# Smaller last additions, landing waits on GpSimd and another closing barrier in a fused SSM and FFN kernel

## The chip, the cores and the metric

The kernel runs on one core of one Trainium2 chip. The metric is device time in microseconds (us) of one execution.

Numbers in ns are starts and durations of the trace's instruction records. "Landing" means the last of the completion events of a store's semaphore in the trace. The profile's views round the same records to 0.01 or 0.1 us.

## The reference, cut to what matters

```
xn = layernorm(x)                                   # x: 2048 x 512, bf16
out = x + ssm(xn) + (silu(xn @ w_gate) * (xn @ w_up)) @ w_down
# ssm: complex diagonal recurrence over the 2048 rows (512 states), then
#      y = 2 * Re(h @ C^T) + xn * Dskip
```

The output is 2048 x 512 in bf16. The kernel handles the rows in four chunks of 512, each of four row tiles of 128.

## The kernel before: the parts that the change and the argument touch

A small scheduler orders tasks for five engines: `pe` (TensorE), `dve` (VectorE), `act` (ScalarE), `pool` (GpSimd) and `sp` (SyncE, which issues nearly all DMAs). The last function computes a chunk's output. For each row tile TensorE accumulates 11 matmuls of the FFN (`mmA`) and 8 of the SSM (`mmB`) in one PSUM bank, VectorE adds the bank to the residual, and SyncE stores the result. In the last chunk the fourth tile is cut in two pieces of 256 columns.

```python
def dc_chunk(c, mid=None, split_last=False):
    ...
    for lt in range(4):
        if split_last and lt == 3:
            items.append((lt, 0, 256))
            items.append((lt, 256, 256))
        else:
            items.append((lt, 0, 512))
    ...
    for (lt, c0, nc_), bk in zip(items, banks):   # mmA: 11 matmuls, hT x wd
        ...
    for (lt, c0, nc_), bk in zip(items, banks):   # mmB: 8 matmuls, hss x W12
        ...
        g.add("dve", lambda e, ...: e.tensor_tensor(out=x_sb[:, a, c0:c0 + nc_],
              in0=pbank[:, bk, 0:nc_], in1=x_sb[:, a, c0:c0 + nc_], op=ALU.add), ...)
        dma("st_out%d_%d" % (a, c0), out_v[:, a, c0:c0 + nc_], x_sb[:, a, c0:c0 + nc_], ...)
```

At the end each engine's stream is emitted into a block. SyncE also waits for every output's landing, and the block closes with a barrier of all engines.

```python
block = es.enter_context(nc.Block())
...
@block.sync
def _(e):
    _emit(e, streams["sp"])
    for t in streams["sp"]:
        if t.out:
            e.wait_ge(t.sem, 16)
...
@block.gpsimd
def _(e):
    _emit(e, streams["pool"])
```

## Time and profile before

| Kernel before | |
|---|---|
| time, median of 3 runs | 180.56 us (180.40 to 181.02) |
| profiled span | 178.8 us |
| TensorE, VectorE busy | 98%, 90% |
| last matmul's end to the span's end ("the tail") | 2.489 us |

The page of the kernel before gives the span, the engines' busy shares (line of its part 1) and, by engine, the chain of waits that ended last (line of its part 4). PE is TensorE's matmuls, PEld its weight loads, DVE VectorE, ACT ScalarE, POOL GpSimd and SP SyncE; a q behind a name is that engine's instruction queue.

```profile
span 178.8 us, 2346 instructions
...
PE 174.5 (98%) x908; PEld 82.9 (46%) x908; DVE 160.6 (90%) x272; ACT 86.5 (48%) x107; POOL 13.0 (7%) x24
...
PE 95%; DMA 2%; ACTq 1%; ACT 0%; DVE 0%; issue 0%
```

TensorE is the chain, nearly from start to end. Of the lines that follow, L713 is the FFN's gate and up matmuls, L900 is `mmA`, L913 `mmB` and L918 the additions; after the change, L901, L914 and L919. An ending can be shortened only behind its last matmul, so that is where to look. The timeline of the kernel before from 176.2 us (start, duration, engine, line, operation, and in brackets the idle time before it and what ended that):

```profile
175.93 1.20 SPq L385 DMA_DIRECT2D out_dram<-x_sb  x2
175.93 0.38 PE L913 MATMUL pb<-W,hss 128*128 128x256 bf16 x2
176.35 0.42 DVE L918 TENSOR_TENSOR x_sb<-pb,x_sb 128x256 bf16<-128x256 f32 x1 [0.45 <-PE pb L913]
```

The last matmul ends at 175.93 + 0.38 = 176.31 us. The last addition follows at 176.35 and takes 0.42 us. The second of the two stores ends its issue at 175.93 + 1.20 = 177.13 us. What follows is in the instructions of SyncE's landing waits (L986) and of the block's close (L272); columns are durations in ns (min/median/max), then the first and last start in us:

```profile
L986 SPq EVENT_SEMAPHORE  x8: 27/28/28, 177.2 to 178.4; - x8
```

```profile
L272 POOLq EVENT_SEMAPHORE  x2: 17/17/17, 178.6 to 178.7; - x2
L272 POOLq DRAIN  x1: 1431/1431/1431, 75.3 to 75.3; - x1
...
L272 SPq COMPARE_BRANCH  x1: 33/33/33, 178.4 to 178.4; - x1
L272 SPq DRAIN  x1: 7/7/7, 178.6 to 178.6; - x1
...
L272 PEldq EVENT_SEMAPHORE  x1: 51/51/51, 178.8 to 178.8; - x1
```

The view lists groups, not an order. In order of time: SyncE's last landing wait ends at 178.4, its branch out of the block follows, its drain at 178.6, GpSimd gathers the engines' signals (178.6) and releases them (178.7), and the others leave by 178.8. GpSimd's own drain is recorded at 75.3 us, where its program ends. Its 1431 ns span GpSimd's last operation (75.37 to 76.70 us in the records), and nobody waits for it.

### The profile page before, as it was taken

The page shows a single profiled execution, that of the slowest core. Times are in us where ns is not written, and L with a number is a line of the kernel's source. Part 1 is how long each engine was busy: PE and PEld are TensorE (multiplying, and loading weights), DVE is VectorE, ACT ScalarE, POOL GpSimd, SP SyncE. Part 2 cuts the span into 40 slices and gives each one's busy share as a digit, 9 for nine tenths or more (in the row PEclk, how much of TensorE's full clock was granted, in tenths as well). Part 3 has the DMA queues.
Part 4 walks back from the last instruction along what each step waited for, and adds up shares of the span by engine and source line. Part 5 has one row for each costly group of instructions (what it writes and reads, how often), then busy time and mean ns, then how long its engine had stood idle before and what let it go on. Part 6 is the DMA issues. An engine that isn't in the chain of part 4 may idle for free.

```text
span 178.8 us, 2346 instructions
## 1 busy us (share of the span) xinstructions
PE 174.5 (98%) x908; PEld 82.9 (46%) x908; DVE 160.6 (90%) x272; ACT 86.5 (48%) x107; POOL 13.0 (7%) x24
## 2 busy tenths in 40 slices
PE   8799999999999999999999999999999999999994
PEld 2594444444444444444444444444444444444643
DVE  3888759998799999999999999999999999999733
ACT  3379899899696992060565651000965620000000
POOL 3362300001300000210000000000000000000000
DMA  5995646669360000002330000001100000001212
GB/s 159 353 355 110 129 81 72 148 170 354 113 117 4 0 0 0 0 0 92 85 64 0 0 0 4 0 0 59 59 0 4 0 0 0 0 0 33 69 48 88
DMA packets 23410, 12.37 MB, mean 69 GB/s; under 512 B 15112, under 2 KB 23400, under 8 KB 23400
## 3 DMA queue, kind: packets, MB, share of 16 engines
q1 hardware_dynamic: 22832, 11.70, 24.6%
q10 hardware_dynamic: 568, 0.53, 1.0%
q8 instruction: 7, 0.11, 0.3%
q14 instruction: 3, 0.02, 0.0%
HBM read 6.46 MB, written 2.10 MB: 48 GB/s over the span
## 4 chain that ended last, share of the span: by engine, by line
PE 95%; DMA 2%; ACTq 1%; ACT 0%; DVE 0%; issue 0%
PE pb L713 36%; PE pb L900 21%; PE pb L913 15%; PE pb L818 15%; PE pb L752 3%; DMA wg<-in_B_w_gate_dram 2%; PE pb L781 2%; PE pb L791 1%; ACTq L385 1%; PE pb L543 0%; ACT xnT L549 0%; DVE x_sb L918 0%; PE pb L457 0%
## 5 line engine op out<-in xcount | busy, mean ns | idle before, releaser
L858 DVE TENSOR_TENSOR_SCAN rot<-sm,car,rot 128x512 bf16<-128x512 f32 x32 | 39.1, 1268 | 0.1
L900 PE MATMUL pb<-wd,hT 128*128 128x512 bf16 (+3 forms) x187 | 38.7, 367 | 0.0
L713 PE MATMUL pb<-xnT,wu 128*128 128x512 bf16 x160 | 37.3, 379 | 0.0
L713 PE MATMUL pb<-xnT,wg 128*128 128x512 bf16 x136 | 32.0, 380 | 0.0
L913 PE MATMUL pb<-W,hss 128*128 128x512 bf16 (+1 forms) x136 | 28.3, 367 | 0.0
L818 PE MATMUL pb<-xnT,BT 128*128 128x512 bf16 x128 | 28.1, 379 | 0.0
L900 PEld LDWEIGHTS pb<-wd,hT 128*128 128x128 bf16 (+1 forms) x187 | 18.2, 97 | 20.1
L725 ACT ACTIVATE sg<-pb 128x1024 bf16<-128x1024 f32 x20 | 20.2, 1021 | 10.5 <-PE pb L713 10.2
L713 PEld LDWEIGHTS pb<-xnT,wu 128*128 128x128 bf16 x160 | 15.5, 98 | 18.9 <-ACT uf L771 0.5
L771 ACT ACTIVATE uf<-pb 128x1024 bf16<-128x1024 f32 x20 | 20.4, 1021 | 7.1 <-PE pb L713 5.7
L713 PEld LDWEIGHTS pb<-xnT,wg 128*128 128x128 bf16 x136 | 13.1, 98 | 16.4 <-issue 0.8
L913 PEld LDWEIGHTS pb<-W,hss 128*128 128x128 bf16 x136 | 13.3, 98 | 14.4
L818 PEld LDWEIGHTS pb<-xnT,BT 128*128 128x128 bf16 x128 | 12.5, 98 | 15.1
L825 ACT ACTIVATE u_sb<-pb 128x1024 bf16<-128x1024 f32 x16 | 16.3, 1025 | 3.9 <-PE pb L818 3.5
L918 DVE TENSOR_TENSOR x_sb<-pb,x_sb 128x512 bf16<-128x512 f32 (+1 forms) x17 | 10.9, 655 | 5.0 <-PE pb L913 5.0
L773 DVE TENSOR_TENSOR hT<-sg,uf 128x1024 bf16<-128x1024 bf16 x20 | 13.4, 677 | 2.1 <-ACT uf L771 2.1
L466 DVE BATCH_NORM_STATS2 st<-x_sb 128x6 f32<-128x512 bf16 x16 | 10.2, 681 | 5.0 <-DMA x_sb<-in_A_x_dram 5.0
L495 ACT ACTIVATE xn_sb<-x_sb,nmr,rstd 128x512 bf16<-128x512 bf16 x8 | 5.9, 802 | 10.5 <-DVE nmr L492 10.5
L800 ACT ACTIVATE sg<-pb 96x1024 bf16<-96x1024 f32 x2 | 2.0, 1019 | 17.4 <-PE pb L781 17.4
L849 DVE TENSOR_TENSOR rot<-rot,sin 128x2048 bf16<-128x2048 bf16 x8 | 9.8, 1219 | 0.0
L849 DVE TENSOR_TENSOR rot<-u_sb,sin 128x2048 bf16<-128x2048 bf16 x8 | 9.7, 1218 | 0.0
L849 DVE TENSOR_TENSOR rot<-u_sb,cosT 128x2048 bf16<-128x2048 bf16 x8 | 9.7, 1215 | 0.0
(71 smaller groups left out, 138.8 us busy)
## 6 DMA issues: line engine op xcount, KB each, us to landing
out_dram<-x_sb SPq DMA_DIRECT2D x15, 128.0 KB, 1.7
x_sb<-in_A_x_dram SPq DMA_DIRECT2D x3, 512.0 KB, 7.5
wd<-in_B_w_down_dram SPq DMA_DIRECT2D x1, 1280.0 KB, 7.0
wu<-in_B_w_up_dram SPq DMA_DIRECT2D x1, 768.0 KB, 6.1
wg<-in_B_w_gate_dram SPq DMA_DIRECT2D x1, 608.0 KB, 7.5
wu<-in_B_w_up_dram SPq DMA_DIRECT2D x1, 608.0 KB, 8.6
x_sb<-in_A_x_dram SPq DMA_DIRECT2D x4, 128.0 KB, 2.8
wg<-in_B_w_gate_dram ACTq DMA_DIRECT2D x2, 256.0 KB, 3.8
```

Of the source, the lines that this page charges most:

```text
L466: return g.add("dve", lambda e, a=a: e.bn_stats(out=st[:, a, :], in_=x_sb[:, a, :]), reads=[("x", a)], writes=[("st", a)], name="bnst%d" % ...
L713: inst = e.matmul(pbank[0:fs, bk, :].rearrange("p (j t) -> p j t", j=4), lhsT=w[:, kt, i * 128:i * 128 + fs], rhs=xnT[:, c % 2, :, kt, :], ...
L725: g.add("act", lambda e: e.activation(out=sg[rows, sl, 0:n, :].rearrange("p a t -> p (a t)"), in_=pair_f32(rows, bk, 512 * n), func=AF.Sil ...
L771: g.add("act", lambda e: e.activation(out=uf[rows, ul, 0:n, :].rearrange("p a t -> p (a t)"), in_=pair_f32(rows, bk, 512 * n), func=AF.Ide ...
L773: g.add("dve", lambda e: e.tensor_tensor(out=hT[rows, hb, i0:i0 + n, :], in0=sg[rows, sl, 0:n, :], in1=uf[rows, ul, 0:n, :], op=ALU.mult), ...
L818: inst = e.matmul(pbank[:, bk, :].rearrange("p (j t) -> p j t", j=4), lhsT=BT[:, ri, kt, pt * 128:(pt + 1) * 128], rhs=xnT[:, c % 2, :, kt ...
L825: g.add("act", lambda e: e.activation(out=u_sb[:, us].rearrange("p r t -> p (r t)"), in_=pair_f32(slice(0, 128), b0), func=AF.Identity), r ...
L849: tt = lambda out, a, b, op, r, w, nm: g.add("dve", lambda e: e.tensor_tensor(out=out, in0=a, in1=b, op=op), reads=r, writes=w, name="%s_% ...
L858: g.add("dve", lambda e, A0=A0, A1=A1, k=k, ri=ri, pt=pt: e.tensor_tensor_scan(out=A1[:, k, ri, :], data0=rr[:, pt:pt + 1].to_broadcast([1 ...
L900: inst = e.matmul(pbank[:, bk, 0:nc_], lhsT=hT[0:fs, hb, i, lt * 128:(lt + 1) * 128], rhs=wd[0:fs, i, c0:c0 + nc_], start=(i == 0), stop=F ...
L913: inst = e.matmul(pbank[:, bk, 0:nc_], lhsT=hss[:, hb, pt, ri, lt * 128:(lt + 1) * 128], rhs=W12[:, ri, pt, c0:c0 + nc_], start=False, sto ...
L918: g.add("dve", lambda e, bk=bk, a=a, c0=c0, nc_=nc_: e.tensor_tensor(out=x_sb[:, a, c0:c0 + nc_], in0=pbank[:, bk, 0:nc_], in1=x_sb[:, a, ...
```

## The change

Three intents: shorten the last addition, from 256 to 128 columns; let GpSimd, which is idle and anyway runs the barrier, wait for the landings; and close the block with the barrier that uses semaphores only and leaves GpSimd's drain out. The last 256 columns are still stored by one DMA.

```diff
-        block = es.enter_context(nc.Block())
+        block = es.enter_context(nc.Block(no_gpsimd_drain=True))
...
-                    items.append((lt, 256, 256))
+                    items.append((lt, 256, 128))
+                    items.append((lt, 384, 128))
...
-                dma("st_out%d_%d" % (a, c0), out_v[:, a, c0:c0 + nc_], x_sb[:, a, c0:c0 + nc_], ...)
+                if nc_ == 128 and c0 == 256:
+                    continue
+                d0, dn = (256, 256) if nc_ == 128 else (c0, nc_)
+                dma("st_out%d_%d" % (a, d0), out_v[:, a, d0:d0 + dn], x_sb[:, a, d0:d0 + dn], ...)
...
         @block.sync
         def _(e):
             _emit(e, streams["sp"])
-            for t in streams["sp"]:
-                if t.out:
-                    e.wait_ge(t.sem, 16)
...
         @block.gpsimd
         def _(e):
             _emit(e, streams["pool"])
+            for t in streams["sp"]:
+                if t.out:
+                    e.wait_ge(t.sem, 16)
```

(Cuts: the estimates that the scheduler uses, and the other engines' streams, which only move in the text.)

More of the change, by code (lines that the diff above doesn't have):

```diff
@@ L902, in dc_chunk @@
                 g.add("pe", mmA, reads=[("hT", hb, i) for i in range(FT)] + [("wd", 0), ("wd", 1)],
-                      writes=BK(bk), name="mm_dA%d_%d" % (4 * c + lt, c0), est=FT * (216 if nc_ == 512 else 110), ninst=FT)
+                      writes=BK(bk), name="mm_dA%d_%d" % (4 * c + lt, c0), est=FT * (216 if nc_ == 512 else nc_ * 0.43), ninst=FT)
             if mid is not None:
@@ L916, in dc_chunk @@
                 g.add("pe", mmB, reads=[("hss", hb, pt) for pt in range(PT)] + [("W", ri, pt) for ri in range(2) for pt in range(PT)],
-                      writes=BK(bk), name="mm_dB%d_%d" % (a, c0), est=2 * PT * (216 if nc_ == 512 else 110), ninst=2 * PT)
+                      writes=BK(bk), name="mm_dB%d_%d" % (a, c0), est=2 * PT * (216 if nc_ == 512 else nc_ * 0.43), ninst=2 * PT)
                 g.add("dve", lambda e, bk=bk, a=a, c0=c0, nc_=nc_: e.tensor_tensor(out=x_sb[:, a, c0:c0 + nc_], in0=pbank[:, bk, 0:nc_], in1=x_sb[:, a, c0:c0 + nc_], op=ALU.add),
-                      reads=BK(bk) + [("x", a)], writes=[("xo", a, c0)], name="oadd%d_%d" % (a, c0), est=(660 if nc_ == 512 else 360))
-                dma("st_out%d_%d" % (a, c0), out_v[:, a, c0:c0 + nc_], x_sb[:, a, c0:c0 + nc_], writes=[("out", a, c0)], nbytes=TILEB * nc_ // 512, reads=[("xo", a, c0)], out_=True)
+                      reads=BK(bk) + [("x", a)], writes=[("xo", a, c0)], name="oadd%d_%d" % (a, c0), est=(660 if nc_ == 512 else 100 + nc_))
+                if nc_ == 128 and c0 == 256:
+                    continue
+                d0, dn = (256, 256) if nc_ == 128 else (c0, nc_)
+                dma("st_out%d_%d" % (a, d0), out_v[:, a, d0:d0 + dn], x_sb[:, a, d0:d0 + dn], writes=[("out", a, d0)], nbytes=TILEB * dn // 512,
+                    reads=[("xo", a, c) for c in ((256, 384) if nc_ == 128 else (c0,))], out_=True)
         if _CFG["warm"]:
```

## The prediction

> **What bounds the kernel now.** The page of before: TensorE is busy 98% of a 178.8 us span; the chain of waits is 95% TensorE; the granted clock is 1.000 (view of cores). The change touches only the tail. From the timeline of the last 10 us, the chain, the barrier line's instructions and the DMA view:
>
> - the last 256-column matmul ends near 176.31 us;
> - the last addition, 128x256, runs 176.35 to 176.77 (0.42 us);
> - its store is issued at 176.8 (0.33 us of queue time) and lands some 1.5 us later (median of the two 64 KB stores); SyncE's last wait ends at 178.4;
> - then SyncE's branch (33 ns), drain (7 ns, at 178.6) and barrier signal, GpSimd's gather and release (178.6, 178.7), and the other engines' release up to 178.8. So about 0.4 us lies between landing and end.
>
> Of the 180.56 us, 1.8 us lie outside the span; I expect them unchanged.
>
> **What the change does, costed.**
>
> 1. *Smaller last addition.* Additions took 0.69 us (512 columns) and 0.425 us (256); a line through both gives 0.29 us for 128 (estimate). The first 128-column one starts 0.45 us before the last matmul ends and is done in time, so the chain loses 0.42 - 0.29 = 0.13 us.
> 2. *More, smaller matmuls.* 19 matmuls of 256 columns become 38 of 128. In before's chain the 256-column ones cost 109.8 ns each (9.54 us less 33 of 215.9 ns, over 22), the 128-column ones of the first stage 55.8 ns (40 in 2.23 us). Each split costs 1.8 ns: +0.03 us. The Trainium skill, "TensorE: Matmul & The Clock Gate", Part 1, gives a warm gap of about 56 ns for 128 columns; this trace agrees.
> 3. *One store of 256 columns, as before.* No change, but 0.1 us sooner.
> 4. *VectorE's order.* The compiled order moves the third chunk's second addition (0.69 us) ahead of the two that write hss. These end near 165.4 instead of 164.8; TensorE needs them at 169.4. The sixth piece's new bank wait is for that moved addition (done near 163.1), over 5 us early. No cost.
> 5. *Waits on GpSimd.* GpSimd is idle after 76.7 us; only the last landing counts. SyncE's branch, drain, signal and the hop to GpSimd leave the chain: I estimate 0.1 to 0.2 us of the 0.4.
> 6. *No GpSimd drain in the barrier.* It took 1.43 us, but at 75.3 us, overlapping GpSimd's last operation: hidden, so no gain. (After the change it would stand behind the landing waits; skipping it avoids a loss.)
>
> Sum: -0.13 + 0.03 - 0.15 = -0.25 us, all on the critical path, 0.14% of the whole. **Predicted 180.3 us, 8 in 10 between 179.9 and 180.65. Faster by over 2%: 0.01; within 2%: 0.98; slower by over 2%: 0.01.**
>
> **What would show each step.** 1: the last two additions at 0.29 us each, the last within 0.05 us of the last matmul's end. 2: 128-column matmuls 55 to 57 ns apart, TensorE's end within 0.1 us of 176.3. 3: landing about 1.5 us after issue. 5: 0.2 to 0.3 us from landing to the span's end, no SyncE instruction in between. 6: no GpSimd drain in the tail.
>
> **What would make it wrong.** GpSimd noticing a landing later than SyncE; the semaphore-only barrier having more hops; a narrow addition having a larger fixed cost than the line says; the time outside the span moving. The spread of before (180.4 to 181.02) is as large as the gain.

## The result, and the profile after

| | before | after |
|---|---|---|
| median of 6 runs, first comparison | 180.70 us | 180.26 us |
| ratio, 95% interval | | 0.9977 [0.9961, 0.9993] |
| profiled span | 178.801 us | 178.432 us |
| tail behind the last matmul | 2.489 us | 2.344 us |

The ratios are from runs of the same rounds. All of them lie within 0.0005 of the ratio of the mean times, but they are not the ratios of the medians quoted.

The page of the changed kernel, same lines:

```profile
span 178.4 us, 2380 instructions
...
PE 174.3 (98%) x919; PEld 83.6 (47%) x927; DVE 160.8 (90%) x273; ACT 86.5 (48%) x107; POOL 12.7 (7%) x24
...
PE 95%; DMA 1%; DVE 1%; issue 1%; ACT 0%; POOL 0%
```

Its timeline from 175.45 us:

```profile
175.23 0.74 DVE L919 TENSOR_TENSOR x_sb<-pb,x_sb 128x256 bf16<-128x256 f32 x2 [0.18 <-PE pb L914]
175.25 0.83 PE L914 MATMUL pb<-W,hss 128*128 128x128 bf16 x12
...
175.69 1.09 SPq L385 DMA_DIRECT2D out_dram<-x_sb  x2
176.12 0.29 DVE L919 TENSOR_TENSOR x_sb<-pb,x_sb 128x128 bf16<-128x128 f32 x1 [0.15 <-PE pb L914]
```

VectorE is idle 0.15 us before the last addition, so the first 128-column addition was indeed done in time. The last one takes 0.29 us instead of 0.42. The close of the changed kernel, GpSimd's landing waits (L1007) and the block's end:

```profile
L1007 POOLq EVENT_SEMAPHORE  x8: 43/43/43, 164.3 to 178.0; - x8
```

```profile
L272 PEldq EVENT_SEMAPHORE  x2: 51/51/51, 176.2 to 178.4; - x2
...
L272 POOLq EVENT_SEMAPHORE  x2: 17/17/17, 178.2 to 178.3; - x2
...
L272 SPq DRAIN  x1: 128/128/128, 176.8 to 176.8; - x1
L272 POOLq COMPARE_BRANCH  x1: 33/33/33, 178.1 to 178.1; - x1
```

No GpSimd drain is left, and SyncE's drain moved up to 176.8. But the branch didn't vanish: it stands at 178.1 on GpSimd now, and the order wait, branch, gather, release is the same as before. From the last landing to the span's end the records give 463 ns before and 457 ns after.

The whole difference of the two spans can be split at points in the records:

| Stretch | before, us | after, us | difference, ns |
|---|---|---|---|
| start to the first matmul of L713 | 13.055 | 12.986 | -69 |
| from there to the last chunk's outputs | 146.620 | 146.410 | -210 |
| the last chunk's matmuls (last stages of L900 and L913; L901 and L914 after) | 16.637 | 16.692 | +55 |
| tail | 2.489 | 2.344 | -145 |
| span | 178.801 | 178.432 | -369 |

Only the last two stretches hold changed instructions: -145 + 55 = -90 ns. The other -279 ns are in unchanged parts. The -210 ns come from one stall of TensorE in the profiled run of before, in the waits of 49 to 52 us (who waited for whom, us in total, times, longest):

```profile
PEld pb L713 <- ACT uf L771: 0.5, 1, 0.5
```

The profile of after has no such line in that stretch. Whether that is chance or a consequence of the change is the first thing to test.

### The profile page after: what moved, and what is told of

Its sections match the earlier page's. It is cut to its first block, busy times and chain, and to the rows that moved or that the text cites. A ratio compares the mean times of both kernels' runs of the same rounds, so it can differ in the third digit from the quotient of the medians. Undisturbed runs are those within 1.5% of the kernel's fastest.

```text
span 178.4 us, 2380 instructions
## 1 busy us (share of the span) xinstructions
PE 174.3 (98%) x919; PEld 83.6 (47%) x927; DVE 160.8 (90%) x273; ACT 86.5 (48%) x107; POOL 12.7 (7%) x24
## 4 chain that ended last, share of the span: by engine, by line
PE 95%; DMA 1%; DVE 1%; issue 1%; ACT 0%; POOL 0%
PE pb L713 36%; PE pb L901 21%; PE pb L818 15%; PE pb L914 15%; PE pb L752 3%; PE pb L781 2%; DMA x_sb<-in_A_x_dram 1%; PE pb L791 1%; PE pb L543 1%; DVE st L466 0%; ACT xnT L549 0%; POOL rstd L478 0%; PE pb L450 0%; DVE xn_sb L485 0%; DVE x_sb L919 0%
## 5 line engine op out<-in xcount | busy, mean ns | idle before, releaser
L901 PE MATMUL pb<-wd,hT 128*128 128x512 bf16 (+3 forms) x194 | 38.1, 355 | 0.2
L713 PE MATMUL pb<-xnT,wu 128*128 128x512 bf16 x160 | 37.3, 379 | 0.0
L713 PE MATMUL pb<-xnT,wg 128*128 128x512 bf16 x136 | 32.0, 379 | 0.0
L914 PE MATMUL pb<-W,hss 128*128 128x512 bf16 (+2 forms) x140 | 28.1, 355 | 0.2
L901 PEld LDWEIGHTS pb<-wd,hT 128*128 128x128 bf16 (+1 forms) x198 | 18.5, 98 | 19.9
L713 PEld LDWEIGHTS pb<-xnT,wu 128*128 128x128 bf16 x160 | 15.6, 98 | 18.6
L713 PEld LDWEIGHTS pb<-xnT,wg 128*128 128x128 bf16 x136 | 13.2, 98 | 16.4 <-issue 0.8
L914 PEld LDWEIGHTS pb<-W,hss 128*128 128x128 bf16 x144 | 13.5, 98 | 14.3
L919 DVE TENSOR_TENSOR x_sb<-pb,x_sb 128x512 bf16<-128x512 f32 (+2 forms) x18 | 10.9, 621 | 4.9 <-PE pb L914 4.9
```

The source lines that it names most:

```text
L713: inst = e.matmul(pbank[0:fs, bk, :].rearrange("p (j t) -> p j t", j=4), lhsT=w[:, kt, i * 128:i * 128 + fs], rhs=xnT[:, c % 2, :, kt, :], ...
L901: inst = e.matmul(pbank[:, bk, 0:nc_], lhsT=hT[0:fs, hb, i, lt * 128:(lt + 1) * 128], rhs=wd[0:fs, i, c0:c0 + nc_], start=(i == 0), stop=F ...
L914: inst = e.matmul(pbank[:, bk, 0:nc_], lhsT=hss[:, hb, pt, ri, lt * 128:(lt + 1) * 128], rhs=W12[:, ri, pt, c0:c0 + nc_], start=False, sto ...
L919: g.add("dve", lambda e, bk=bk, a=a, c0=c0, nc_=nc_: e.tensor_tensor(out=x_sb[:, a, c0:c0 + nc_], in0=pbank[:, bk, 0:nc_], in1=x_sb[:, a, ...
```

## The experiments

Theory A: the tail gain is the shorter addition alone, the new ending is worth nothing, and the rest of the measured gain is chance in the kernel's first third. Theory B, the prediction's: the ending is worth another 0.1 to 0.2 us.

All tails, in ns, from the records. They add up from left to right.

| Run | matmul end to last addition | last addition | addition end to issue | issue to landing | landing to end | tail |
|---|---|---|---|---|---|---|
| before | 37 | 425 | 28 | 1536 | 463 | 2489 |
| before_again | 37 | 425 | 28 | 1537 | 463 | 2490 |
| end_only | 38 | 425 | 27 | 1534 | 457 | 2481 |
| split_only | 37 | 291 | 28 | 1536 | 458 | 2350 |
| after | 37 | 292 | 28 | 1530 | 457 | 2344 |
| after_again | 38 | 293 | 28 | 1532 | 466 | 2357 |
| pool_drain | 38 | 291 | 28 | 1534 | 540 | 2431 |
| sp_semonly | 37 | 290 | 27 | 1533 | 542 | 2429 |
| late_wait | 38 | 293 | 28 | 1532 | 68 | 1959 |
| late_again | 37 | 292 | 28 | 1531 | 67 | 1955 |
| late_two_stores | 38 | 293 | 116 | 1534 | 67 | 2048 |
| narrow64 | 80 | 214 | 27 | 1527 | 466 | 2314 |
| late_narrow | 78 | 215 | 28 | 1532 | 67 | 1920 |

All outputs are right.

### split_only: the smaller additions alone

```diff
 # against the changed kernel
-        block = es.enter_context(nc.Block(no_gpsimd_drain=True))
+        block = es.enter_context(nc.Block())
 # and the landing waits back from GpSimd to SyncE
```

> Only the smaller additions; landing waits stay on SyncE and the barrier keeps GpSimd's drain. The tail from TensorE's last matmul end to the span's end took 2.489 us in the kernel before and 2.344 us in the changed one. Theory A (the whole tail gain is the shorter last addition, 0.425 to 0.292 us): tail 2.34 to 2.37 us, that is 0.12 to 0.15 less than before; about 0.46 us from the last landing to the span's end. Theory B (my prediction: moving the waits and the barrier is worth another 0.1 to 0.2 us): this kernel keeps most of the old ending, tail at or above 2.44 us. Both expect a time within 0.2% of the kernel before, and 128-column matmuls 55 to 57 ns apart.

Measured: tail 2.350 us, landing to end 0.458 us, 180.76 us median of 4 runs, ratio 1.0003 [0.9971, 1.0035]. The last addition, from the timeline of this run:

```profile
176.67 0.29 DVE L919 TENSOR_TENSOR x_sb<-pb,x_sb 128x128 bf16<-128x128 f32 x1 [0.15 <-PE pb L914]
```

With the old ending in place, 139 of the 145 ns are there. Theory A holds in the trace.

### end_only: the new ending alone

```diff
 # against the kernel before
-        block = es.enter_context(nc.Block())
+        block = es.enter_context(nc.Block(no_gpsimd_drain=True))
 # and the landing waits from SyncE to GpSimd; pieces stay 256 and 256
```

> Only the ending: landing waits on GpSimd and the semaphore-only barrier; two pieces of 256 columns as in the kernel before. Theory A: tail 2.47 to 2.50 us, no gain against 2.489; from the last landing to the span's end 0.45 to 0.47 us as before (0.463). Theory B: tail 2.29 to 2.39 us, landing to end 0.26 to 0.36 us.

Measured: tail 2.481 us (8 ns less than before), landing to end 0.457 us, ratio 0.9995 [0.9963, 1.0028]. Theory B falls. The landing waits (L1002) and the branch are on GpSimd here, as in the changed kernel:

```profile
L1002 POOLq EVENT_SEMAPHORE  x8: 43/43/43, 168.7 to 178.7; - x8
```

```profile
L272 POOLq COMPARE_BRANCH  x1: 32/32/32, 178.8 to 178.8; - x1
```

This run also shows the stall near 50 us, in the waits of 40 to 60 us:

```profile
PEld pb L713 <- ACT uf L771: 0.9, 1, 0.9
...
PE pb L713 <- ACT uf L771: 0.4, 1, 0.4
```

So the stall comes with the new ending too, and the second profile of the kernel before (below) doesn't have it. Two runs of one program show it best: late_again (below) has the 0.5 us wait and a middle that is 0.21 us longer, and late_wait, the same program, has a wait of 0.4 us and only 0.035 us. The stall goes with the run, not with the kernel. What brings it on was not investigated.

### pool_drain: landing waits on GpSimd, ordinary barrier

```diff
 # against the changed kernel
-        block = es.enter_context(nc.Block(no_gpsimd_drain=True))
+        block = es.enter_context(nc.Block())
```

> The changed kernel with the ordinary barrier: landing waits on GpSimd, followed by GpSimd's drain. Both theories expect the drain to appear at the tail now, behind the last landing wait, instead of hidden near 75 us. If the drain waits only for GpSimd's own old work it costs under 0.1 us there (tail 2.34 to 2.44 us); if it has a large cost of its own, as its 1.43 us record near 75 us might suggest, the tail is 0.5 us longer or more.

Measured: tail 2.431 us, ratio 0.9995 [0.9968, 1.0021]. Of the block's close:

```profile
L272 POOLq COMPARE_BRANCH  x1: 41/41/41, 178.1 to 178.1; - x1
L272 POOLq DRAIN  x1: 46/46/46, 178.2 to 178.2; - x1
```

The drain is now at the end and costs 540 - 457 = 83 ns from landing to end (74 against the 466 of after_again, whose branch took 41 ns as here), of which its own record is 46. The 1431 ns at 75.3 us were GpSimd's unfinished work, not a price of the drain.

### sp_semonly: landing waits on SyncE, semaphore-only barrier

```diff
 # against the changed kernel: only the waits move back
         @block.sync
         def _(e):
             _emit(e, streams["sp"])
+            for t in streams["sp"]:
+                if t.out:
+                    e.wait_ge(t.sem, 16)
```

> The changed kernel with the landing waits back on SyncE, the semaphore-only barrier kept. Theory A: the two engines are alike as waiters; tail 2.34 to 2.42 us, the difference being SyncE's drain and one more hop to GpSimd, of 0.03 to 0.07 us. Theory B: the tail is 0.1 to 0.2 us longer than the changed kernel's 2.344, that is 2.44 to 2.54 us.

Measured: tail 2.429 us, ratio 1.0001 [0.9974, 1.0027]. Both ranges are narrowly missed: theory A's ended at 2.42, theory B's began at 2.44. From landing to end it took 542 ns, 79 more than with the ordinary barrier on the same engine (463). First the line of SyncE's semaphore instructions in the kernel before (only its release), then the lines of the close of this run (the signal at 178.5, and the release):

```profile
L272 SPq EVENT_SEMAPHORE  x1: 17/17/17, 178.7 to 178.7; - x1
```

```profile
L272 SPq EVENT_SEMAPHORE  x2: 17/17/17, 178.5 to 178.6; - x2
...
L272 SPq COMPARE_BRANCH  x1: 33/33/33, 178.3 to 178.3; - x1
L272 SPq DRAIN  x1: 7/7/7, 178.4 to 178.4; - x1
```

By the records' operands, SyncE's drain itself raises the gather's semaphore in the ordinary barrier. In the semaphore-only barrier a separate semaphore instruction does so; it starts 60 ns after the drain's end and ends 77 ns after it. That is the 79 ns, within 2.

The four corners, landing to end in ns, now explain why the new ending gained nothing (540 and 542 are one profile each):

| | ordinary barrier | semaphore-only barrier |
|---|---|---|
| SyncE waits | 463, 458, 463 | 542 |
| GpSimd waits | 540 | 457, 457, 466 |

Each half of the change alone loses about 80 ns, for different reasons: a drain that is no longer hidden, or a signal that no longer rides on the drain. The two together lose neither and come back to where the kernel before was. Step by step, again in ns:

| Step | before | after |
|---|---|---|
| landing to the end of the wait's record | 45 | 67 |
| to the end of the branch's record | 73 | 77 |
| to GpSimd's gather | 162 | 128 |
| gather, release, other engines leave | 183 | 185 |

SyncE's drain, signal and hop to GpSimd were worth only 162 - 128 = 34 ns, and GpSimd gives 26 of those back in its own wait and branch.

### after_again: the changed kernel once more

> The changed kernel once more. Theory A (the tail is fixed, and what moves from run to run is the head): tail 2.34 to 2.35 us and 0.45 to 0.46 us from landing to end, as in the first profile; TensorE's last stage takes the same time within 0.02 us; the span may differ by up to 0.6 us, all of it before TensorE's last stages. The ratio to the kernel before lies between 0.998 and 1.0005: 0.145 us gained in the tail less 0.055 us lost in the smaller matmuls is 0.09 us or 0.05%. Theory B (the first comparison's 0.23% is real): ratio 0.996 to 0.9985.

Measured: tail 2.357 us, landing to end 0.466 us, last chunk's matmuls 16.691 us (16.692 the first time), 180.80 us median of 6 runs, ratio 0.9998 [0.9978, 1.0019]. Theory A's range for the ratio holds; the 0.23% of the first comparison doesn't come back. Three of its narrower ranges were missed, each by little: the tail (2.34 to 2.35), landing to end (0.45 to 0.46) and the span, which was to differ by up to 0.6 us. The span was 179.132 us, 0.700 more than the first profile of the very same program. Of that, 0.687 us lie before the first matmul of L713 (13.673 instead of 12.986 us), while the inputs load.

### before_again: the kernel before once more

> The kernel before once more, profiled again, since its tail is known from one profile alone. Theory A (the tail is fixed, the head moves): tail from TensorE's last end to the span's end 2.47 to 2.50 us (2.489 in the first), landing to end 0.455 to 0.47 us; the second pieces' 256-column matmuls 109 ns apart. Theory B (the tail of before varies as much as its times do, by 0.5 us or more): tail outside 2.40 to 2.58. The ratio to itself lies within 0.2% of 1; what it shows beyond that is chance.

Measured: tail 2.490 us, landing to end 0.463 us, last chunk's matmuls 16.637 us, to the nanosecond as before. From the first matmul of L713 to the last matmul's end it took 163.048 us instead of 163.257: the stall of 0.21 us is absent. The changed kernel took 163.102 us in that stretch, in both of its profiles. So the unchanged middle of the two kernels is equal, and the 54 to 55 ns between them are those of the last chunk's smaller matmuls. The ratio of this kernel to itself was 0.9989 [0.9967, 1.0012], which shows what chance does here.

### late_wait: the last two landing waits behind the barrier

The branch and the barrier need 0.39 us, but no data from the last store. So they can run while it is in flight.

```diff
 # against the changed kernel; outs = the output stores in order of issue
         @block.gpsimd
         def _(e):
             _emit(e, streams["pool"])
-            for t in streams["sp"]:
-                if t.out:
-                    e.wait_ge(t.sem, 16)
+            for t in outs[:-2]:
+                e.wait_ge(t.sem, 16)
+
+    for t in outs[-2:]:                    # after the block is closed
+        nc.gpsimd.wait_ge(t.sem, 16)
```

> The changed kernel, with the waits for the last two output landings moved from inside the block to behind its barrier (still on GpSimd, so nothing ends before the data has landed). Four profiles so far put 0.457 to 0.463 us between last landing and span's end where the ending is whole, nearly all of it branch and barrier. Theory A (the barrier can run while the store is in flight): barrier done near 1.2 us after TensorE's end, landing to end 0.06 to 0.12 us, tail 1.93 to 2.00 us instead of 2.344, and the time 0.2 to 0.3% below the kernel before, ratio 0.9965 to 0.9985. Theory B (the end of the run waits for something the span doesn't show, as the 1.76 us outside the span suggest): the span shrinks by the 0.39 us but the time outside it grows by as much, and the ratio stays at 0.9985 to 1.001.

Measured: tail 1.959 us, landing to end 0.068 us, 180.14 us median of 6 runs against 180.86 of before in the same rounds, ratio 0.9965 [0.9942, 0.9987]. The trace accounts for 530 - 51 = 479 ns, or 0.27%, of that 0.35%, well inside the interval. The landing wait (L1011) and the close:

```profile
L1011 POOLq EVENT_SEMAPHORE  x1: 43/43/43, 178.5 to 178.5; - x1
```

```profile
L272 POOLq EVENT_SEMAPHORE  x2: 17/17/17, 177.5 to 177.6; - x2
...
L272 POOLq COMPARE_BRANCH  x1: 41/41/41, 177.3 to 177.3; - x1
```

The barrier is over by 177.7 us, the data lands at 178.43, one semaphore instruction ends the span. Outside the span this kernel spends 1.74 to 1.81 us (in late_again), the kernel before 1.69 to 1.77 (in before_again): 0.05 us more on average (0.03 against the other runs of before in these rounds), not the 0.39 that theory B expected. The spans of these executions are on record to 0.1 us only.

### late_two_stores: and the last 256 columns in two stores

```diff
 # against late_wait: every piece has its own store, also those of 128 columns
-                if nc_ == 128 and c0 == 256:
-                    continue
-                d0, dn = (256, 256) if nc_ == 128 else (c0, nc_)
 # and the last three landings are awaited behind the barrier
```

> As the late wait, with the last 256 columns stored as two stores of 128 columns (32 KB each), one behind each addition. Theory A (landing time of a small store is nearly all fixed): issue to landing stays at 1.5 us, from 1.45 to 1.55, tail within 0.06 us of the late-wait kernel's. Theory B (a smaller last store lands sooner in proportion to its bytes): 1.3 us or less, tail 0.2 us shorter. A queue time of 0.33 us for each issue leaves room for both stores, so no issue should wait for the one before.

Measured: tail 2.048 us, ratio 0.998 [0.9954, 1.0006]. The sizes and times to landing, from the DMA view (KB each, median us):

```profile
out_dram<-x_sb SPq DMA_DIRECT2D x1, 64.0 KB, 1.5
out_dram<-x_sb SPq DMA_DIRECT2D x2, 32.0 KB, 1.5
```

Half the bytes land no sooner: 1534 ns after issue, against 1532. So far theory A. But the tail is 89 ns longer than late_wait's, outside its range of 60, because the last sentence was wrong: a store of 256 bytes per partition kept SyncE's queue busy for 430 ns (both did), one of 512 bytes for 332. The view of the output's stores (duration ns min/median/max) has both:

```profile
L385 SPq DMA_DIRECT2D out_dram<-x_sb x18: 332/332/430, 80.2 to 176.9; - x18
```

The second store's issue therefore waited for the first, and began 116 ns after the addition's end instead of 28. Those 88 ns are the loss.

### narrow64: last pieces of 256, 192 and 64 columns

```diff
 # against the changed kernel
-                    items.append((lt, 256, 128))
-                    items.append((lt, 384, 128))
+                    items.append((lt, 256, 192))
+                    items.append((lt, 448, 64))
```

> The changed kernel with the last three pieces 256, 192 and 64 columns. The line through 0.69, 0.425 and 0.292 us puts the 64-column addition at 0.225 us: 0.067 less on the chain. Theory A (a matmul of under 128 columns costs no less than one of 128, about 54 to 56 ns, since each has its own weight load): TensorE's end comes 0.4 to 0.55 us later counted from the start of its last stage, more than the addition gives back; the kernel is 0.3 to 0.5 us slower than the changed one in span less start jitter. Theory B (a 64-column matmul costs half of one of 128, near 29 ns): TensorE's end unchanged, but the 192-column addition then ends some 0.15 us after the last matmul and holds back the last one, so the tail is 2.40 to 2.45 us.

Measured: tail 2.314 us, 30 ns less than the changed kernel; the last chunk's matmuls 16.688 us, the same; ratio 0.9982 [0.9952, 1.0012], too wide to say more. Neither theory had it whole. On TensorE theory B was right: the matmuls of 192 columns started 82.5 ns apart and those of 64 columns 29, each with its own weight load. On VectorE it was wrong, as the timeline shows:

```profile
175.80 0.49 DVE L919 TENSOR_TENSOR x_sb<-pb,x_sb 128x192 bf16<-128x192 f32 x2 [0.23 <-PE pb L914]
```

Two additions of 357 and 214 ns take 490 together. The second starts 82 ns before the first one's record ends, so the first holds it up by 43 ns (80 instead of 37 behind the matmul) and not by the 125 or more that the records' lengths suggest.

### late_again and late_narrow: does the better version hold, and do the gains add?

late_again is late_wait without an edit. late_narrow has the edits of late_wait and narrow64 together:

```diff
 # against late_wait
-                    items.append((lt, 256, 128))
-                    items.append((lt, 384, 128))
+                    items.append((lt, 256, 192))
+                    items.append((lt, 448, 64))
```

> The late wait once more. Theory A: tail 1.95 to 1.97 us, landing to end 0.065 to 0.07 us, ratio to the kernel before 0.9965 to 0.9985: 0.53 us less tail and 0.055 us more in TensorE's smaller matmuls make 0.475 us, or 0.26%. Theory B (the first ratio, 0.9965, was chance and the time outside the span pays the gain back): ratio above 0.9985 and over 1.9 us outside the span instead of 1.8.

> The late wait with the last pieces of 256, 192 and 64 columns: both gains together. Theory A (they add, since the addition lies before the store's issue and the barrier beside its flight): tail 1.92 to 1.94 us, 0.03 less than the late wait alone, too little to see in the times; ratio to the kernel before 0.996 to 0.9985. Theory B (the barrier's steps, which don't move, become the last to end): the gain of the narrow piece is lost, tail 1.95 us or more. TensorE's 64-column matmuls again 29 ns apart.

Measured: late_again tail 1.955 us, ratio 0.9967 [0.9949, 0.9985]; late_narrow tail 1.920 us, ratio 0.9972 [0.9951, 0.9994]. The late wait holds. The narrow piece adds its 35 ns in the trace, as theory A expected, and the times can't resolve it.

## Why the prediction was right or wrong

The time, 180.26 us, was inside the range and close to the 180.3 predicted. But two of the terms were mis-sized, and the agreement owes something to chance.

1. *The smaller last addition:* right. Predicted 0.42 to 0.29 us, measured 425 to 292 ns, in every run with the split.
2. *More, smaller matmuls:* right in kind, too small. Predicted "Each split costs 1.8 ns: +0.03 us"; the last chunk's matmuls took 55 ns more, 2.9 ns for each of the 19 splits. The Trainium skill, "TensorE: Matmul & The Clock Gate", section "Back-to-back issue gap", gives N / 2.4 + 2.5 ns for the warm gap of an isolated matmul of N columns. The records of this stream agree: 55.8 ns at 128 columns and 29 at 64, and about 109 at 256. By that formula each split costs another 2.5 ns, which makes an estimate of 48 ns. My 109.8 ns for 256 columns came from an average over a stage with its boundaries in it, and that hid part of the cost.
3. *One store as before:* right, 1536 and 1530 ns from issue to landing.
4. *VectorE's order:* right. The two additions that write hss (the SSM's states) end at 164.85 us in the profile after, 4 us before TensorE's first matmul that reads them, at 168.98.
5. *Waits on GpSimd:* this is the step that failed. "SyncE's branch, drain, signal and the hop to GpSimd leave the chain: I estimate 0.1 to 0.2 us of the 0.4." Measured: 6 ns (463 to 457), less than the 9 ns by which this stretch differs between the two profiles of the changed kernel; the sign that the prediction named, 0.2 to 0.3 us from landing to end, didn't appear. The branch doesn't leave, it moves to GpSimd; drain, signal and hop were worth 34 ns; and GpSimd's wait and branch are 26 ns slower. I had summed records on the old path without asking which of them the new path has again. One of the risks that I listed came in, without a cost beside it: GpSimd's wait ends 67 ns after the landing, SyncE's ended after 45. The rule for that was at hand: list the new chain too, record by record.
6. *No GpSimd drain:* right, and shown. It was hidden before; placed behind the landing waits it cost 74 to 83 ns (pool_drain).

With its terms measured, the change is worth 145 - 55 = 90 ns, or 0.05%, not 0.25 us. The first comparison showed 0.23% with an interval that just excludes 0.05% (0.9993 at its upper end); the second, with the same two kernels, showed 0.02% with one that includes it. The traces assign the 279 ns above the change's own part, in the first pair of profiles, to the start and to one stall that comes and goes with the run. What makes the start vary by up to 0.7 us between runs of one program (12.82 to 13.95 us over all thirteen profiles) was not investigated.

## What to carry to other kernels

List the chain of the ending in both versions before costing a change to it: an instruction that leaves one engine's stream is no gain if another engine's stream has it again. Work that needs no data from the last store, such as the closing barrier, belongs beside its flight, with only the landing wait behind it: here that gave 0.39 us in the trace, over four times what the change itself gave. The Trainium skill, "DMA: Bandwidth & Descriptors", section "Rules for kernel authors", gives the same advice for compute, to wait on a DMA's semaphore late; late_wait and late_again show that it holds for the end of a kernel too.

## What the Trainium skill lacked or had wrong

- "TensorE: Matmul & The Clock Gate", "Back-to-back issue gap": it gives about 81 ns for 128 columns and 131 ns for 512 in a stream of weight loads and matmuls, and calls N / 2.4 + 2.5 ns the isolated gap. In the last chunk's streams, with a weight load for every matmul, the gaps were 29, 55.8, 82.5, 109 and 216 ns for 64, 128, 192, 256 and 512 columns. The formula holds for the stream, and the other two figures don't appear.
- "Advanced Engine Details and Errata", "Control Flow Timing", gives about 108 ns for a compare-and-branch. At the block's end the record was 32 to 41 ns, but the next instruction of that engine started 156 to 170 ns after the branch's start (runs with the whole ending inside the block).
- "DMA: Bandwidth & Descriptors", "Anatomy of one DMA — SWDGE (gpsimd) path", gives a fixed cost of about 2.0 us for DMAs that GpSimd issues. That section has no figure for SyncE's queue. The last stores from that queue landed 1.53 us after issue, at 32 KB and at 64 KB alike.
- No page that I read has the queue time of a store by the bytes it takes per partition: 332 ns at 512 bytes, 430 ns at 256.
- No page that I read has the cost of closing a block: 0.46 us from landing to the end, 74 to 83 ns for a GpSimd drain that isn't hidden, 79 ns for the semaphore-only barrier when SyncE comes last.
- "VectorE: DVE Perf Modes", "The DRAIN you can't avoid", says that the next operation doesn't start until the pipe is empty, and that one which isn't held starts earlier. That section has no number for how much earlier. Here the next addition's record began 82 ns before the end of the one before.
